# Attention scores and states' read by single heads in a fused attention and two-layer MoE kernel

## The chip, the cores and the metric

The kernel runs on one core of a Trainium2 chip. The metric is the device time of one execution in microseconds (us). The kernel before takes 1207.65 us, the median of 3 runs (1207.26 to 1207.77).

The engines are TensorE (PE, with its weight loads listed as PEld), VectorE (DVE), ScalarE (ACT), GpSimd (POOL) and SyncE (SP), which here only issues DMAs.

## The reference, cut to what matters

For each of 8 batches and 8 heads there are 512 tokens `x` and 32 states, each of 64 numbers. Tokens read the states, and the states read the tokens; both go on into two dense blocks.

```python
B, H, S, D = x.shape                      # 8, 8, 512, 64;  state: 8, 8, 32, 64
scores = scale * x @ state^T              # 512 x 32, softmax over the 32 states
xread  = softmax(scores) @ state
scores2 = scale * state @ x^T             # 32 x 512, softmax over the 512 tokens
sread  = softmax(scores2) @ x
h = concat([xread, sread], axis=2)        # 544 rows a head
# heads side by side: 4096 rows of tokens and 256 of states, 512 wide
y = ((h @ w1) * (h @ w2)) @ w3 @ w_out    # first block
g = y @ w_in;  out = (g * clip(g + 3, 0, 6) / 6) @ w_out2
```

`scores2` is the transpose of `scores`, so the kernel computes one product for both.

## The kernel before, in words

**The whole.** A first stage (0 to about 107 us) loads and unpacks weights and multiplies `w3` with `w_out` (line 463), while the attention of batches 0 and 1 is done in small pieces between the weights. Then a main loop runs over the batches b, and in each over 8 slots m of the first block's width. A slot has 12 matmuls for `ps_ab` (lines 88 to 90, `mm3`: three products of rounded halves instead of one in full precision), a product of the two halves on ACT and DVE (`asb`, `ab`, lines 571 and 573), its split into a high part `abh` (ACT) and a low part `abl` (DVE), and 12 matmuls into `x2` with it, one slot or two later. After batch 7 comes `s_block` for the states' 256 rows, then the second dense block (lines 996, 1158), which fills the rest of the span.

**The attention.** `attention(b)` is a generator. The main loop of batch b advances `attention(b + 1)` by one step at a time: after the `ps_ab` matmuls of a slot, and in the middle of a slot's `x2` matmuls. For batches 0 and 1 (`fine`) the steps are called from the first stage. Its parts, in order:

- `scores(g)` for a half g of the heads (four heads, two pairs): one matmul for each pair of heads. The stationary operand is a block diagonal `br[:, c, :]` of 128 rows (two heads' 64 numbers) and 64 columns (two heads' 32 states), the moving one `xr[:, c, :]` with 512 tokens. Two pairs make up one PSUM bank. For each half, `scores_out` takes the maximum on DVE, transposes 32x32 blocks on DVE for the tokens' own softmax (`sN`), and on ACT writes the exponentials `e2` and their sum `r2`.
- `max_n`, `exp_n`, `sum_n`, `div_n`: the tokens' softmax. `exp_n` also divides the states' exponentials: two ACT instructions of 128x512 (line 294) multiply `e2` with `1 / sum`.
- `e2_t`: eight TensorE transpositions of 128x128 turn `e2` into two banks `ps_e`, which ACT copies to `e2t` (tokens on partitions).
- `sread`: 32 matmuls into one bank `ps_r`. Stationary is `xn` (128 tokens x 64 numbers of one head), moving is `e2t` (128 tokens x 32 states). `sread_out` copies the bank to `xs` on ACT, and SP stores it; for batch 7 it goes to `xs_r`, which is split at once into `xs_hl`, the operand of `s_block`.

`p_mm(v)` multiplies a batch's states with `w1` and `w2`; its matmuls are 64 rows by 32 columns with 256 moving columns, eight of which stand beside each other in the array, and they use `br` too. Its results `ps_p` are split into `ph` (ACT) and `pl` (DVE).

**The order.** All engines run their instructions in the order in which the code writes them. PSUM has 8 banks: four for accumulation (`acc`: `ps_w`, `x2`), and a pool "b" of four, from which `ps_ab`, `ps_s`, `ps_e`, `ps_r`, `ps_p` and `ps_sb` take a bank as soon as an older tile's last reader is done. A step that holds a bank longer moves the tiles behind it to other banks.

A matmul in full 32-bit floats shows as two records in the trace; so `scores` of one batch are 8 records, `sread` 64, a `p_mm` 32. A transposition is one record.

Of the kernel before, what the change touches and what calls it, by code (L numbers as in the profile page):

```python
# [7 lines left out]
F32 = mybir.dt.float32  # L8
# [4 lines left out]
AF = mybir.ActivationFunctionType  # L13
# [3 lines left out]
DRAM = bass.MemoryType.DRAM  # L17


def attn_moe_kernel(tc, xt_d, xn_d, bd_d, wa, wb, wc, wi, wo, out):  # L20

# [15 lines left out]
    nc = tc.nc  # L39
    B, H, S, D, NS = 8, 8, 512, 64, 32  # L40
    DM, F1, F2 = 512, 1024, 2048
    T = S // 128
# [4 lines left out]
    scale = 1.0 / float(D) ** 0.5  # L47
# [5 lines left out]
    def open_pool(key, **kw):  # L53
        es[key] = ExitStack()
        return es[key].enter_context(tc.tile_pool(name=key, **kw))
# [10 lines left out]
    def bank(name):  # L66
        return psum.tile([128, 512], F32, tag="b", name=name, bufs=4)
# [32 lines left out]
    w12 = {}  # L100
# [7 lines left out]
    mid = open_pool("mid", bufs=1, side=left)  # L108
    ident = mid.tile([128, 128], F32, name="ident")
    att = open_pool("att", bufs=1, side=right)  # L110
# [99 lines left out]
    x_t, A_t, st_t = {}, {}, {}  # L210
    xs_r, xs_hl = None, []
    room = 0

    def load_x(b):
        xr = att.tile([128, 4, 512], F32, tag="xr", name=f"xr{b}")
        br = mid.tile([128, 4, 64], F32, tag="br", name=f"br{b}", bufs=2)
        nc.sync.dma_start(out=br, in_=bd_d[b])
        nc.sync.dma_start(out=xr, in_=xt_d[b])
        x_t[b] = (xr, br)

    def attention(b, fine=False):

        xr, br = x_t.pop(b)
        st_t[b] = br
        xn = att.tile([128, T, DM], F32, tag="xn", name="xn")
        nc.sync.dma_start(out=xn, in_=xn_d[b])
        sN = att.tile([128, 2, 512], F32, tag="sN", name="sN")
        e2 = att.tile([128, 2, 512], F32, tag="e2", name="e2")
        mr = att.tile([128, 32], F32, tag="mr", name="mr", bufs=2)
        m2, r2 = mr[:, :2], mr[:, 2:4]  # L230

        def scores(g):

            ps = bank("ps_s")
            for j in range(2):
                c = 2 * g + j
                nc.tensor.matmul(ps[64 * j:64 * j + 64], br[:, c, :], xr[:, c, :], start=True, stop=True)  # L237
            return ps

        def scores_out(g, ps):  # L240
            nc.vector.tensor_reduce(out=m2[:, g:g + 1], in_=ps, op=ALU.max, axis=AX.X)
            nc.vector.tensor_scalar(out=m2[:, g:g + 1], in0=m2[:, g:g + 1], scalar1=-scale, scalar2=None, op0=ALU.mult)
            nc.vector.transpose(out=sN[:, g, :], in_=ps)
            nc.scalar.activation(out=e2[:, g, :], in_=ps, func=AF.Exp, bias=m2[:, g:g + 1], scale=scale,
                                 accum_out=r2[:, g:g + 1])
# [12 lines left out]

        def sread():
            ps = bank("ps_r")  # L260
            for c in range(4):
                g, j = divmod(c, 2)
                for t in range(T):
                    for r in range(2):
                        h = 64 * r
                        o = 64 * j + NS * (r ^ g)
                        nc.tensor.matmul(ps[h:h + 64, c * NS:(c + 1) * NS], xn[:, t, c * 128 + h:c * 128 + h + 64],  # L267
                                         e2t[:, t, g, o:o + NS], start=(t == 0), stop=(t == T - 1))
            return ps

        def sread_out(ps):
            if b == B - 1:
                nc.scalar.copy(out=xs_r[:, :, b * NS:], in_=ps[:, :4 * NS].rearrange("p (c n) -> p c n", c=4))
                t = att.tile([128, T, DM], F32R, tag="xn", name="xs_hl").rearrange("p (i a) f -> p i (a f)", i=2)
                xs_hl.extend(t[:, i].rearrange("p (k f) -> p k f", k=KD) for i in range(2))
                rnd(xs_hl[0], xs_r, "A")
                rest(xs_hl[1], xs_r, xs_hl[0], "V")
                return
            xs = att.tile([128, 4, NS], F32, tag="xs", name="xs")
            nc.scalar.copy(out=xs.rearrange("p c n -> p (c n)"), in_=ps[:, :4 * NS])  # L280
            nc.sync.dma_start(out=xsd[:, :, b * NS:(b + 1) * NS], in_=xs)

        def max_n():
# [6 lines left out]

        def exp_n():
            nc.scalar.activation(out=sN, in_=sN, func=AF.Exp, scale=scale)
            for g in range(2):
                nc.scalar.activation(out=e2[:, g, :], in_=e2[:, g, :], func=AF.Copy, scale=r2[:, g:g + 1])

        def sum_n():
            nc.vector.tensor_reduce(out=sm[:, :, 0], in_=sv, op=ALU.add, axis=AX.X)
# [11 lines left out]
        sv = sN.rearrange("p g (k n) -> p (g k) n", n=NS)  # L309
        yield  # L310
        if fine:
            ps = scores(0)
            yield
            scores_out(0, ps)
            yield
            ps = scores(1)
            yield
            scores_out(1, ps)
        else:
            ps = [scores(g) for g in range(2)]  # L320
            for g in range(2):
                scores_out(g, ps[g])
            yield
# [7 lines left out]
        e2t = att.tile([128, T, 2, 128], F32, tag="xtl", name="e2t")  # L331
        sm = att.tile([128, 32, 1], F32, tag="sm", name="sm", bufs=2)
        if fine:
            ps = e2_t(0)
            yield
            e2_out(0, ps)
            sum_n()
            yield
            ps = e2_t(1)
            yield  # L340
            e2_out(1, ps)
            div_n()
            yield
            ps = sread()
            yield
            sread_out(ps)
            aT = att.tile([128, 2, 512], F32, tag="e2", name="aT")
            turn(aT)
        else:
            sum_n()  # L350
            yield
            div_n()
            yield
            yield
            ps = [e2_t(u) for u in range(2)]
            for u in range(2):
                e2_out(u, ps[u])
            yield
            aT = att.tile([128, 2, 512], F32, tag="e2", name="aT")
            turn(aT)  # L360
# [7 lines left out]
        rest(A_l, aT, A_h, "V")  # L368
        if not fine:
            yield  # L370
            sread_out(sread())

    live = []

# [11 lines left out]
    with tc.manual_schedule():  # L386
        make_identity(nc, ident)
        ps = bank("ps_i")
# [10 lines left out]
        def p_mm(v):  # L399
            b, mm = divmod(v, 4)  # L400
            ps = p_ps[v] = [bank("ps_p") for c in range(2)]

            for i in range(2):
                o = 512 * i + 256 * (mm % 2)
                for q in range(4):
                    for c in range(2):
                        j, k = divmod(q, 2)
                        r = slice(64 * (k ^ c), 64 * (k ^ c) + 64)
                        nc.tensor.matmul(ps[c][32 * q:32 * q + 32, 256 * i:256 * i + 256],  # L409
                                         st_t[b][r, 2 * c + j, 32 * k:32 * k + 32],  # L410
                                         w12[mm // 2, 2 * c + j][r, o:o + 256], start=True, stop=True)

        def p_split(v):
            ps = p_ps.pop(v)
# [384 lines left out]
        for b in range(B):  # L799
# [15 lines left out]
            for m in range(0 if b else 4, M1):  # L815
# [22 lines left out]
                if b == B - 2 and m >= 2:  # L838
                    if m == 2:
                        xs_r = wsq.tile([128, KD, SR], F32, name="xs_r")  # L840
                        n = (B - 1) * NS
# [124 lines left out]
        st = {}  # L966
# [306 lines left out]
def _layout(x, state, moe_w1, moe_w2, moe_w3, moe_w_out, moe2_w_in, moe2_w_out):  # L1273
    import numpy as np

    def words(a):
        return np.ascontiguousarray(a).view(np.uint64)

    B, H, S, D = x.shape
    NS = state.shape[2]  # L1280

    x6 = x.reshape(B, 4, 2, 4, 128, D)
    xt = x6.transpose(0, 2, 5, 1, 3, 4).reshape(B, 128, 4, 512)
    xn = x6.transpose(0, 4, 3, 1, 2, 5).reshape(B, 128, 4, 512)
    st = state.reshape(B, 4, 2, NS, D).transpose(0, 2, 4, 1, 3)
    bd = np.zeros((B, 2, D, 4, 2, NS), state.dtype)
    for c in range(4):
        for r in range(2):
            bd[:, r, :, c, r ^ c // 2, :] = st[:, r, :, c, :]
    wa = moe_w_out.reshape(4, 2, 128, 512).transpose(0, 2, 1, 3).reshape(4, 128, 1024)  # L1290
    w3t = moe_w3.T.reshape(8, 128, 2, 4, 128)
    wb = np.concatenate([w3t[:, :, 0].reshape(4, 2, 128, 512).transpose(0, 2, 1, 3).reshape(4, 128, 1024),
                         w3t[:, :, 1].transpose(2, 1, 0, 3).reshape(4, 128, 1024)])
    w12 = np.stack([moe_w1, moe_w2]).reshape(2, 4, 128, 2, 512)
    wc = w12.transpose(3, 1, 2, 0, 4).reshape(2, 4, 128, 1024)
    wi = moe2_w_in.reshape(2, 2, 128, 2, 8, 128).transpose(4, 2, 3, 0, 1, 5)
    wo = moe2_w_out.reshape(2, 8, 128, 4, 2, 2, 32).transpose(1, 2, 4, 0, 5, 3, 6).reshape(8, 128, 2, 2, 2, 128)
    wi, wo = (np.stack([w[:, :, 0, 1], w[:, :, 1, 1], w[:, :, 0, 0], w[:, :, 1, 0]], 2).reshape(8, 128, 1024)
              for w in (wi, wo))
    return {  # L1300
        "xt": np.ascontiguousarray(xt), "xn": np.ascontiguousarray(xn),
        "bd": bd.reshape(B, 128, 4, 64),
        "wa": words(wa), "wb": words(wb), "wc": words(wc), "wi": words(wi), "wo": words(wo),
    }

# [18 lines left out]
```

## Time and profile before

| What | Value |
|---|---|
| Median of 3 runs | 1207.65 us |
| The profiled execution | 1205.57 us |
| Its span, first to last instruction | 1203.8 us |
| PE busy | 1185.6 us, 98% of the span |
| DVE busy | 862.1 us, 72% |
| ACT busy | 553.5 us, 46% |
| Mean share of the 16 DMA engines, main loop from 220 us | 54% |
| Granted clock of TensorE | 0.996 |

Busy time of PE is made from ends that are modelled, so where instructions stand close the time of a group is read from its first start to the start of what follows. Time that an engine waits stands in brackets behind a row, with the engine and tile that ended the wait.

### The profile page before, as it was taken

How to read it: one execution, taken by the hardware profiler on the slowest of the kernel's cores; microseconds unless marked ns; L12 is line 12 of the kernel's file. 1: busy time of each engine (PE TensorE's matmuls, PEld its weight loads, DVE VectorE, ACT ScalarE, POOL GpSimd, SP SyncE). 2: the span in 40 equal slices, each digit the busy share in tenths (PEclk: the TensorE clock that was granted, in tenths of full speed). 3: DMA queues.
4: the chain of work that ended last, by engine and by line, in shares of the span. 5: the costliest groups of instructions: out<-in, count | busy, mean ns of one | idle time of the engine just before them, and what ended most of it. 6: DMA issues, size and time to landing. Idle time of an engine off the chain costs nothing.

```text
span 1203.8 us, 17243 instructions
## 1 busy us (share of the span) xinstructions
PE 1185.6 (98%) x6734; PEld 944.4 (78%) x6734; DVE 862.1 (72%) x1230; ACT 553.5 (46%) x811; POOL 44.6 (4%) x59
## 2 busy tenths in 40 slices
PE   7999999999999999999999999999999999999997
PEld 4356777777777789888888888888888888888887
DVE  7997888897898663455677866688567886558483
ACT  3544556455555553344445434454344543334341
POOL 0000000000000000000101001010010100001100
PEclk8999999999999999999999999999999999999999
DMA  8773558576674502036989769897698976536973
GB/s 328 270 252 109 182 169 283 184 267 212 206 269 167 180 1 70 19 105 222 314 240 303 232 215 298 249 293 248 219 284 258 277 251 205 176 123 178 246 224 71
DMA packets 118930, 252.67 MB, mean 210 GB/s; under 512 B 45248, under 2 KB 63168, under 8 KB 112448
## 3 DMA queue, kind: packets, MB, share of 16 engines
q1 hardware_dynamic: 109552, 222.46, 54.1%
q0 software_dynamic: 7632, 27.79, 11.4%
q10 hardware_dynamic: 1664, 1.31, 0.3%
q8 instruction: 53, 0.87, 0.3%
q14 instruction: 29, 0.24, 0.1%
HBM read 182.39 MB, written 47.64 MB: 191 GB/s over the span
## 4 chain that ended last, share of the span: by engine, by line
PE 91%; DVE 5%; DMA 2%; ACT 1%; issue 0%; SPq 0%; ACTq 0%
PE ps L996 25%; PE ps_d L1158 25%; PE x L88 5%; PE x L89 5%; PE x L90 5%; PE ps_ab L88 4%; PE ps_ab L89 4%; PE ps_ab L90 4%; PE ps_p L409 2%; PE ps_w L463 2%; PE ps_hs L996 2%; PE ps_so L1171 2%; DMA raw<-in_wb_dram 1%; PE ps_r L267 1%; PE ps_s L237 1%; DMA swih<-sh 1%
## 5 line engine op out<-in xcount | busy, mean ns | idle before, releaser
L996 PE MATMUL ps<-xc,wah 128*128 128x512 f32 x512 | 157.8, 389 | 0.0
L79 DVE TENSOR_TENSOR hlj<-g,hlj 128x1024 fp32r<-128x1024 f32 x84 | 102.4, 1219 | 36.7 <-ACT hlj L71 33.6
L926 ACT ACTIVATE rl<-c,half 128x512 f32<-128x512 f32 x96 | 69.5, 724 | 117.0 <-DVE c L896 68.1
L996 PE MATMUL ps<-xc,wbh 128*128 128x512 f32 x384 | 118.2, 389 | 0.0
L1158 PE MATMUL ps_d<-hlj,wah 128*128 128x512 f32 x384 | 118.2, 389 | 0.0
L88 PE MATMUL x<-abh,w3ph 128*128 128x512 f32 (+1 forms) x288 | 112.2, 390 | 1.5 <-ACT abh L71 1.5
L71 ACT ACTIVATE hlj<-g 128x1024 fp32r<-128x1024 f32 x84 | 88.5, 1058 | 52.1 <-PE ps_d L1158 46.6
L996 PEld LDWEIGHTS ps<-xc,wah 128*128 128x128 f32 x512 | 95.7, 188 | 19.5
L89 PE MATMUL x<-abl,w3ph 128*128 128x512 f32 (+1 forms) x288 | 109.0, 378 | 0.2 <-DVE abl L79 0.2
L90 PE MATMUL x<-abh,w3pl 128*128 128x512 f32 (+1 forms) x288 | 108.9, 378 | 0.0
L89 PE MATMUL ps_ab<-Al,ph 128*128 128x512 f32 x256 | 99.8, 390 | 0.6 <-DVE Al L79 0.6
L88 PE MATMUL ps_ab<-Ah,ph 128*128 128x512 f32 x256 | 100.3, 392 | 0.0
L90 PE MATMUL ps_ab<-Ah,pl 128*128 128x512 f32 x256 | 99.7, 389 | 0.0
L996 PE MATMUL ps<-xc,wal 128*128 128x512 f32 x256 | 99.6, 389 | 0.0
L1158 PE MATMUL ps_d<-hlj,wbh 128*128 128x512 f32 x288 | 88.7, 389 | 0.0
L71 ACT ACTIVATE abh<-ab 128x512 fp32r<-128x512 f32 (+1 forms) x72 | 43.7, 607 | 88.9 <-DVE ab L573 88.9
L1158 PEld LDWEIGHTS ps_d<-hlj,wah 128*128 128x128 f32 x384 | 72.1, 188 | 15.0
L996 PEld LDWEIGHTS ps<-xc,wbh 128*128 128x128 f32 x384 | 72.0, 188 | 14.9
L573 DVE TENSOR_TENSOR ab<-ps_ab,asb 128x512 f32<-128x512 f32 x64 | 44.1, 689 | 46.2 <-PE ps_ab L90 43.0
L964 POOL DMA_DIRECT2D g<-g x41 | 35.6, 869 | 1074.9 <-DVE c L896 566.8
L996 PE MATMUL ps<-xc,wbl 128*128 128x512 f32 x192 | 74.7, 389 | 0.0
L1158 PE MATMUL ps_d<-hlj,wal 128*128 128x512 f32 x192 | 74.7, 389 | 0.0
(170 smaller groups left out, 2357.6 us busy)
## 6 DMA issues: line engine op xcount, KB each, us to landing
g<-g POOLq DMA_DIRECT2D x41, 512.0 KB, 6.9
wah<-swih SPq DMA_DIRECT2D x32, 512.0 KB, 4.2
wal<-swil SPq DMA_DIRECT2D x32, 512.0 KB, 5.4
wah<-swoh SPq DMA_DIRECT2D x32, 512.0 KB, 4.4
wal<-swol SPq DMA_DIRECT2D x32, 512.0 KB, 5.3
wbh<-swih SPq DMA_DIRECT2D x32, 384.0 KB, 5.0
wbl<-swil SPq DMA_DIRECT2D x32, 384.0 KB, 5.3
wbh<-swoh SPq DMA_DIRECT2D x32, 384.0 KB, 5.7
```

What stands on the lines that cost most here:

```text
L71: nc.scalar.activation(out=out_, in_=in_, func=AF.Copy)
L79: e.tensor_tensor(out=out_, in0=in_, in1=hi.bitcast(F32), op=ALU.subtract)
L88: nc.tensor.matmul(ps, lh, rh, start=first, stop=False)
L89: nc.tensor.matmul(ps, lh, rl, start=False, stop=False)
L90: nc.tensor.matmul(ps, ll, rh, start=False, stop=last)
L409: nc.tensor.matmul(ps[c][32 * q:32 * q + 32, 256 * i:256 * i + 256], st_t[b][r, 2 * c + j, 32 * k:32 * k + 32], w12[mm // 2, 2 * c + j][r, ...
L463: nc.tensor.matmul(w3_ps[m], t[:, o:o + 128], wout[k], start=k == 0, stop=k == M1 - 1)
L573: nc.vector.tensor_tensor(out=ab[:, :n], in0=psb[:, :n], in1=a[:, :n], op=ALU.mult)
L926: nc.scalar.activation(out=rl, in_=c, func=AF.Relu, bias=half, scale=sign / 6.0)
L964: nc.gpsimd.dma_start(out=to, in_=of, accum_op=ALU.add)
L996: nc.tensor.matmul(ps, u[:, k, :], v[:, k, :], start=first and k == 0 and i == 0, stop=k == 1 and i == 2, skip_group_check=True)
L1158: nc.tensor.matmul(d[name][q][:, f], a, x[:, k, f], start=i < 3 and n == 0 and z == 0, stop=n == NG - 1 and z == 2, skip_group_check=True)
```

## The change

The first operand list loses the block diagonal: `br` holds only the states (128 partitions x 4 pairs x 32 columns), so its DMA brings 512 bytes instead of 1 KB to a partition. Scores are computed head by head with eight matmuls on 64x32 tiles: row half r of the array and column group c; row half r writes bank r. Both halves are computed together, for batches 0 and 1 too. A bank now holds the heads of equal r, four of them.

The states' read has stationary and moving operand exchanged: stationary is a head's `e2t` (128 tokens x 32 states), moving its `xn` (128 x 64), four heads beside each other in the four column groups. It uses undivided exponentials. The division is done when the result (128x128) is copied out of PSUM (`sread_div`, two ACT instructions of 128x64), and one step later a TensorE transposition puts it into the second quarter of the same bank, from where it goes on as before. The two ACT instructions on `e2` in `exp_n` go. `p_mm` keeps shape and number of its matmuls, with the new places of heads.

```diff
-        br = mid.tile([128, 4, 64], F32, tag="br", name=f"br{b}", bufs=2)
+        br = mid.tile([128, 4, NS], F32, tag="br", name=f"br{b}", bufs=2)
...
-        def scores(g):
-            ps = bank("ps_s")
-            for j in range(2):
-                c = 2 * g + j
-                nc.tensor.matmul(ps[64 * j:64 * j + 64], br[:, c, :], xr[:, c, :], start=True, stop=True)
+        def scores():
+            ps = [bank("ps_s") for r in range(2)]
+            for c in range(4):
+                for r in range(2):
+                    h = slice(64 * r, 64 * r + 64)
+                    nc.tensor.matmul(ps[r][NS * c:NS * c + NS], br[h, c, :], xr[h, c, :], start=True, stop=True)
...
         def sread():
             ps = bank("ps_r")
-            for c in range(4):
-                g, j = divmod(c, 2)
+            for g in range(2):
                 for t in range(T):
-                    for r in range(2):
-                        h = 64 * r
-                        o = 64 * j + NS * (r ^ g)
-                        nc.tensor.matmul(ps[h:h + 64, c * NS:(c + 1) * NS], xn[:, t, c * 128 + h:c * 128 + h + 64],
-                                         e2t[:, t, g, o:o + NS], start=(t == 0), stop=(t == T - 1))
+                    for c in range(4):
+                        nc.tensor.matmul(ps[NS * c:NS * c + NS, 64 * g:64 * g + 64], e2t[:, t, g, NS * c:NS * c + NS],
+                                         xn[:, t, 128 * c + 64 * g:128 * c + 64 * g + 64], start=(t == 0),
+                                         stop=(t == T - 1))
             return ps
 
-        def sread_out(ps):
+        def sread_div(ps):
+            sr = att.tile([128, 128], F32, tag="sr", name="sr")
+            for g in range(2):
+                nc.scalar.activation(out=sr[:, 64 * g:64 * g + 64], in_=ps[:, 64 * g:64 * g + 64], func=AF.Copy,
+                                     scale=r2[:, g:g + 1])
+            return sr
+
+        def sread_out(ps, sr):
+            ps = ps[:, 128:256]
+            nc.tensor.transpose(ps, sr, ident)
...
         def exp_n():
             nc.scalar.activation(out=sN, in_=sN, func=AF.Exp, scale=scale)
-            for g in range(2):
-                nc.scalar.activation(out=e2[:, g, :], in_=e2[:, g, :], func=AF.Copy, scale=r2[:, g:g + 1])
...
         if not fine:
             yield
-            sread_out(sread())
+            ps = sread()
+            sr = sread_div(ps)
+            yield
+        sread_out(ps, sr)
```

Three places show what this does to the order of the instructions. The first is PE in batch 4's main loop, where the scores of batch 5 follow a `p_mm`; before, these are its rows from the last `p_mm` matmul on:

```order
L409 MATMUL ps_p_2756<-big3_504,br4_2005 32x256
L237 MATMUL ps_s_2779<-xr5_2560,br5_2561 64x512 [waits DMAHW4_49,DMAHW3_49,Activation_49]
L237 MATMUL ps_s_2779<-xr5_2560,br5_2561 64x512
L237 MATMUL ps_s_2782<-xr5_2560,br5_2561 64x512 [waits DVE_49]
L237 MATMUL ps_s_2782<-xr5_2560,br5_2561 64x512
L88 MATMUL x2_2_2342<-abh_2593,w3ph6_494 128x512
```

The same place now:

```order
L416 MATMUL ps_p_2786<-big3_506,br4_2025 32x256
L238 MATMUL ps_s_2809<-xr5_2586,br5_2587 32x512 [waits DMAHW4_49,DMAHW3_49,Activation_49]
L238 MATMUL ps_s_2810<-xr5_2586,br5_2587 32x512 [waits DVE_49]
L238 MATMUL ps_s_2809<-xr5_2586,br5_2587 32x512
L238 MATMUL ps_s_2810<-xr5_2586,br5_2587 32x512
...
L88 MATMUL x2_2_2368<-abh_2619,w3ph6_496 128x512
```

Four matmuls of 64 columns became eight of 32, in the tile shape of the `p_mm` ahead of them, and the wait for DVE (its `ab` of the slot, which reads the bank that is taken) moved from the third matmul to the second.

The second place is PE at the states' read of batch 5, later in the same loop; before, from the read to the start of the next slot's `x2`:

```order
L267 MATMUL ps_r_3173<-e2t_2959,xn_2737 64x32 [waits DMAHW3_49,Activation_49]
L267 MATMUL ps_r_3173<-e2t_2959,xn_2737 64x32 x31
...
L88 MATMUL ps_ab0_3224<-Ah_2547,ph_3036 128x512 [waits DVE_49]
...
L88 MATMUL ps_ab1_3231<-Ah_2547,ph_3036 128x512 [waits Activation_49]
...
L88 MATMUL x2_0_2894<-abh_3096,w3ph5_432 128x512
```

The same place now:

```order
L265 MATMUL ps_r_3205<-xn_2767,e2t_2991 32x64 [waits DMAHW3_49,Activation_49]
L265 MATMUL ps_r_3205<-xn_2767,e2t_2991 32x64 x31
...
L88 MATMUL ps_ab0_3256<-Ah_2573,ph_3068 128x512 [waits DVE_49]
...
L88 MATMUL ps_ab1_3263<-Ah_2573,ph_3068 128x512 [waits DVE_49]
...
L279 MATMUL ps_r_3205<-ident_73,sr_3238 128x128 [waits Activation_49]
L88 MATMUL x2_0_2926<-abh_3128,w3ph5_434 128x512
```

The transposition stands behind six `x2` and twelve `ps_ab` matmuls, and `ps_r` keeps its bank until then; the second `ps_ab` therefore takes the bank of `ps_p` and waits for DVE (its first `pl`), where it waited for ACT's copy of `ps_r`.

The third place is ACT around the same read, before:

```order
L71 ACTIVATE ph_3167<-ps_p_3150 128x512 [waits PE_49]
L280 COPY xs_3206<-ps_r_3173 128x128 [waits PE_49]
L571 COPY asb_3238<-ps_ab0_3224 128x512 [waits PE_49,Activation_49]
L71 ACTIVATE sh_3245<-w_2981 128x768 [waits DMAHW0_49,DMAHW1_49,DVE_49,Activation_49]
```

And now:

```order
L71 ACTIVATE ph_3199<-ps_p_3182 128x512 [waits PE_49]
L273 ACTIVATE sr_3238<-ps_r_3205,mr_2771 128x64 [waits PE_49]
L273 ACTIVATE sr_3238<-ps_r_3205,mr_2771 128x64
L577 COPY asb_3270<-ps_ab0_3256 128x512 [waits PE_49,Activation_49]
L288 COPY xs_3275<-ps_r_3205 128x128 [waits PE_49]
L71 ACTIVATE sh_3281<-w_3013 128x768 [waits DMAHW0_49,DMAHW1_49,DVE_49,Activation_49]
```

The copy of the read result moved behind the slot's `asb` and waits for the transposition; `sh` (a part of a weight's split, which has nothing to do with attention) is queued behind it.

## Rows read from the trace of the kernel before

**Rows 1.** Windows of the span: length, busy us and count by engine, clock, DMA.

```profile
core 0: us, PE busy (x) PEld busy (x) DVE busy (x) ACT busy (x) POOL busy (x), PEclk, DMA share, GB/s
...
73.00:106.00 33.00, 31.72 (x204) 19.95 (x202) 29.97 (x44) 12.62 (x22) 0.00 (x0) 1.00 0.48 169
...
173.00:220.00 47.00, 45.74 (x368) 34.59 (x367) 41.32 (x67) 25.17 (x42) 0.00 (x0) 1.00 0.69 231
220.00:455.00 235.00, 235.00 (x1784) 181.57 (x1783) 188.03 (x292) 128.53 (x209) 0.00 (x0) 1.00 0.54 182
```

**Rows 2.** Waits of PE: line waited for, total us, times, longest.

```profile
PE ps_ab L89 <- DVE Al L79: 0.6, 1, 0.6
```

**Rows 3.** Timeline, first stage's end: start, us, engine, line, out<-in [idle <-releaser].

```profile
105.16 0.69 DVE L573 TENSOR_TENSOR ab<-ps_ab,asb 128x512 f32<-128x512 f32 x1
106.56 0.49 PE L88 MATMUL x<-abh,w3ph 128*128 128x512 f32 x1 [1.46 <-ACT abh L71]
```

**Rows 4.** Timeline of PE, scores of half a batch (batch 1).

```profile
87.90 1.08 PE L237 MATMUL ps_s<-xr,br 128*64 128x512 f32 x4 [0.39 <-PE ps_ab L90]
88.91 0.50 PE L88 MATMUL x<-abh,w3ph 128*128 128x512 f32 x1
```

**Rows 5.** Timeline of PE, p_mm and the scores of batch 2.

```profile
137.10 1.09 PE L409 MATMUL ps_p<-big,br 64*32 64x256 f32 x32
138.13 1.94 PE L237 MATMUL ps_s<-xr,br 128*64 128x512 f32 x8
140.00 0.50 PE L88 MATMUL x<-abh,w3ph 128*128 128x512 f32 x1
```

**Rows 6.** Timeline of 137.10 to 137.16 us alone: that p_mm's first starts.

```profile
137.10 0.45 PE L409 MATMUL ps_p<-big,br 64*32 64x256 f32 x8
```

**Rows 7.** Timeline of all engines at the states' read of batch 5.

```profile
338.62 2.06 PE L267 MATMUL ps_r<-e2t,xn 128*64 128x32 f32 x64
340.61 0.50 PE L88 MATMUL x<-abh,w3ph 128*128 128x512 f32 x1
340.76 1.28 DVE L79 TENSOR_TENSOR pl<-ps_p,ph 128x512 fp32r<-128x512 f32 x2
342.10 0.40 PE L88 MATMUL ps_ab<-Ah,ph 128*128 128x512 f32 x1
```

**Rows 8.** Timeline of PE, four transpositions among ps_ab matmuls (batch 1).

```profile
117.00 0.39 PE L90 MATMUL ps_ab<-Ah,pl 128*128 128x512 f32 x1
117.23 0.60 PE L252 MATMUL ps_e<-ident,e 128*128 128x128 f32 x4
117.58 0.47 PE L88 MATMUL ps_ab<-Ah,ph 128*128 128x512 f32 x1
117.90 0.39 PE L89 MATMUL ps_ab<-Al,ph 128*128 128x512 f32 x1
```

**Rows 9.** Timeline of DVE behind batch 1's states' read.

```profile
125.90 1.29 DVE L79 TENSOR_TENSOR pl<-ps_p,ph 128x512 fp32r<-128x512 f32 x2 [1.29 <-ACT ph L71]
```

**Rows 10.** Timeline of ACT, DVE and PE between 173 and 220 us.

```profile
187.57 0.85 ACT L71 ACTIVATE sh<-w 128x768 fp32r<-128x768 f32 x1 [2.50 <-DMA swih<-sh]
...
204.56 1.32 ACT L294 ACTIVATE e<-e,mr 128x512 f32<-128x512 f32 x2
...
208.11 0.69 DVE L79 TENSOR_TENSOR abl<-ab,abh 128x512 fp32r<-128x512 f32 x1 [1.76 <-ACT abh L71]
...
219.40 0.66 PE L252 MATMUL ps_e<-ident,e 128*128 128x128 f32 x4 [1.26 <-DVE ab L573]
```

**Rows 11.** Timeline of DVE and PE at batch 4's transpositions.

```profile
261.97 0.69 DVE L79 TENSOR_TENSOR abl<-ab,abh 128x512 fp32r<-128x512 f32 x1 [0.80 <-ACT abh L71]
...
271.44 0.68 DVE L573 TENSOR_TENSOR ab<-ps_ab,asb 128x512 f32<-128x512 f32 x1
...
272.42 1.09 PE L252 MATMUL ps_e<-ident,e 128*128 128x128 f32 x8
```

**Rows 12.** Timeline at the start of s_block.

```profile
447.49 1.06 ACT L71 ACTIVATE xs_hl<-xs_r 128x1024 fp32r<-128x1024 f32 x1
...
448.58 1.22 DVE L79 TENSOR_TENSOR xs_hl<-xs_r,xs_hl 128x1024 fp32r<-128x1024 f32 x1 [1.42 <-ACT xs_hl L71]
...
454.14 0.28 PE L89 MATMUL ps_sb<-xs_hl,wsh 128*128 128x256 f32 x1
```

More of the change, by code (lines that the diff above doesn't have):

```diff
@@ L17, with attn_moe_kernel @@
 DRAM = bass.MemoryType.DRAM
-def attn_moe_kernel(tc, xt_d, xn_d, bd_d, wa, wb, wc, wi, wo, out):
+def attn_moe_kernel(tc, xt_d, xn_d, st_d, wa, wb, wc, wi, wo, out):
     nc = tc.nc
@@ L215, in load_x @@
         xr = att.tile([128, 4, 512], F32, tag="xr", name=f"xr{b}")
-        br = mid.tile([128, 4, 64], F32, tag="br", name=f"br{b}", bufs=2)
-        nc.sync.dma_start(out=br, in_=bd_d[b])
+        br = mid.tile([128, 4, NS], F32, tag="br", name=f"br{b}", bufs=2)
+        nc.sync.dma_start(out=br, in_=st_d[b])
         nc.sync.dma_start(out=xr, in_=xt_d[b])
@@ L260, in sread @@
             ps = bank("ps_r")
-            for c in range(4):
-                g, j = divmod(c, 2)
+            for g in range(2):
                 for t in range(T):
-                    for r in range(2):
-                        h = 64 * r
-                        o = 64 * j + NS * (r ^ g)
-                        nc.tensor.matmul(ps[h:h + 64, c * NS:(c + 1) * NS], xn[:, t, c * 128 + h:c * 128 + h + 64],
-                                         e2t[:, t, g, o:o + NS], start=(t == 0), stop=(t == T - 1))
-            return ps
-        def sread_out(ps):
+                    for c in range(4):
+                        nc.tensor.matmul(ps[NS * c:NS * c + NS, 64 * g:64 * g + 64], e2t[:, t, g, NS * c:NS * c + NS],
+                                         xn[:, t, 128 * c + 64 * g:128 * c + 64 * g + 64], start=(t == 0),
+                                         stop=(t == T - 1))
+            return ps
+        def sread_div(ps):
[7 more added lines that the diff above has]
+            nc.tensor.transpose(ps, sr, ident)
             if b == B - 1:
-                nc.scalar.copy(out=xs_r[:, :, b * NS:], in_=ps[:, :4 * NS].rearrange("p (c n) -> p c n", c=4))
+                nc.scalar.copy(out=xs_r[:, :, b * NS:], in_=ps.rearrange("p (c n) -> p c n", c=4))
                 t = att.tile([128, T, DM], F32R, tag="xn", name="xs_hl").rearrange("p (i a) f -> p i (a f)", i=2)
@@ L279, in sread_out @@
             xs = att.tile([128, 4, NS], F32, tag="xs", name="xs")
-            nc.scalar.copy(out=xs.rearrange("p c n -> p (c n)"), in_=ps[:, :4 * NS])
+            nc.scalar.copy(out=xs.rearrange("p c n -> p (c n)"), in_=ps)
             nc.sync.dma_start(out=xsd[:, :, b * NS:(b + 1) * NS], in_=xs)
@@ L311, in attention @@
         if fine:
-            ps = scores(0)
+            ps = scores()
             yield
-            scores_out(0, ps)
+            scores_out(0, ps[0])
             yield
-            ps = scores(1)
             yield
-            scores_out(1, ps)
+            scores_out(1, ps[1])
         else:
-            ps = [scores(g) for g in range(2)]
+            ps = scores()
             for g in range(2):
@@ L345, in attention @@
             yield
-            sread_out(ps)
+            sr = sread_div(ps)
             aT = att.tile([128, 2, 512], F32, tag="e2", name="aT")
@@ L370, in attention @@
             yield
-            sread_out(sread())
+            ps = sread()
+            sr = sread_div(ps)
+            yield
+        sread_out(ps, sr)
     live = []
@@ L404, in p_mm @@
                 o = 512 * i + 256 * (mm % 2)
[L405 to L411, printed above, removed]
+                for c in range(4):
+                    for r in range(2):
+                        h = slice(64 * r, 64 * r + 64)
+                        nc.tensor.matmul(ps[r][NS * c:NS * c + NS, 256 * i:256 * i + 256], st_t[b][h, c, :],
+                                         w12[mm // 2, c][h, o:o + 256], start=True, stop=True)
         def p_split(v):
@@ L1284, in _layout @@
     xn = x6.transpose(0, 4, 3, 1, 2, 5).reshape(B, 128, 4, 512)
[L1285 to L1289, printed above, removed]
+    st = state.reshape(B, 4, 2, NS, D).transpose(0, 2, 4, 1, 3).reshape(B, 128, 4, NS)
     wa = moe_w_out.reshape(4, 2, 128, 512).transpose(0, 2, 1, 3).reshape(4, 128, 1024)
@@ L1301, in _layout @@
         "xt": np.ascontiguousarray(xt), "xn": np.ascontiguousarray(xn),
-        "bd": bd.reshape(B, 128, 4, 64),
+        "st": np.ascontiguousarray(st),
         "wa": words(wa), "wb": words(wb), "wc": words(wc), "wi": words(wi), "wo": words(wo),
```

## The prediction

> **What bounds the kernel now.** I read the table by windows first. From 220 to 455 us PE is busy in 235.00 of 235.00 us, beside DVE with 188.03 [rows 1]: what PE saves there shortens the run, as long as DVE follows. The window 73 to 106 reads otherwise: DVE 29.97 of 33.00, PE 31.72 [rows 1], where "busy" PE is mostly PE early; its end shows who decides, since DVE multiplies `ab` at 105.16 and PE then stands 1.46 us until 106.56 for the high part of it [rows 3]. The window 173 to 220 has PE at 45.74 of 47.00; the missing time is one wait, 1.26 us before transpositions at 219.40, ended by DVE's `ab` [rows 1, 10]. From the list of waits, one more counts: 0.6 us for `Al` at 133 us [rows 2]. So PE's savings count at full price from 106.6 us on, except between 173 and 219.4, where another chain decides.
>
> **Scores.** Eight records in tiles of two took 138.13 to 140.00 = 1.87 us, four rounds [rows 5]; four records, two rounds, took 87.90 to 88.91 = 1.01 [rows 4]. The difference gives 0.43 us for a round of 512 columns and 0.15 fixed. Now eight tiles of 64x32 are to stand in one round: two rounds (two records a matmul) instead of four, -0.86. That eight such tiles do run together is in the trace: `p_mm` has this tile shape, eight of its records start within 60 ns [rows 6], and all 32 of 256 columns take 137.10 to 138.13 = 1.03 us [rows 5], which is four rounds at half of 0.43 and about 0.17 fixed. The scores now follow a `p_mm` of their own shape, so up to 0.17 more may go where the shape no longer changes; I take half: **-0.95 a batch**, bounds 0.86 to 1.03.
>
> It counts for batch 2 (138 us) and batches 4 to 7. For batches 0 and 1 it falls into the stretch before 106 us that DVE sets, for batch 3 (191 us) into the other chain: 0. Five times 0.95 = **-4.75**. The second bank's wait for DVE `ab` stands in front now; at batch 3 it may bind, under cover of that chain, and elsewhere `ab` is out before the `p_mm` ahead is through.
>
> **States' read.** 64 records took 338.62 to 340.61 = 1.99 us [rows 7]: 32 rounds of two tiles, (1.99 - 0.15) / 32 = 57 ns a round, though only 32 columns stream in each. Now four column groups with 64 columns make 16 rounds. A round's floor by streaming is 0.43 x 64 / 512 = 54 ns; I take 57, the round that is there: 16 x 57 ns + 0.15 = 1.06, **-0.93 a batch**. Here the shape (128 rows, 32 columns) isn't in the trace. Its nearest rows are the present two tiles of 128 rows side by side, and the four column groups of `p_mm`. Bounds: no gain (31 ns a record as now) and -0.93.
>
> The Trainium skill's page "TensorE: Matmul & The Clock Gate", section "Wait — 56ns, not 53.3ns?", states that matmul starts never come closer than some 25 ns however few columns stream. By that, 64 records would take 1.6 us and the gain would be 0.24 instead of 0.93. The eight starts within 60 ns [rows 6] speak against this rule for records on different tiles, so I don't follow it.
>
> It counts for batch 1 (120.5 us) and batches 3 to 7, six times, **-5.58**. At batch 1 the time is kept, though PE waits for `Al` behind it: that chain begins with DVE standing 1.29 us for `ph`, made from the `p_mm` behind the read [rows 9], so it moves along. Batch 0 is under DVE, batch 2 (177 us) in the other chain.
>
> **The transposition.** One more full-array instruction a batch. Four of them, from 117.23, with the longer step behind them (117.58 to 117.90 instead of 0.23) cost 0.35 + 0.09 = 0.44, 0.11 each [rows 8]. A lone one pays more of what is fixed: 0.2, bounds 0.11 and 0.44. It counts for batches 3 to 7, **+1.00**; that of batch 1 falls into the 0.6 us of [rows 2], those of 0 and 2 are covered. Its input, ACT's two copies of 128x64, has the six `x2` and twelve `ps_ab` matmuls of some 4 us ahead of it.
>
> **The held bank.** `ps_r` stays a step longer, so the second `ps_ab` takes the bank of the first `ps_p` and waits for DVE's first `pl`. At batch 5 DVE did both from 340.76 in 1.28, so the first ended near 341.4. The first `ps_ab` began at 342.10 [rows 7] and the second six matmuls of 0.23 later, 343.5; 0.93 earlier it is 342.5. That leaves 1.1 us: 0.
>
> **ACT's division.** Two instructions, 1.32 us [rows 10], go from each `exp_n`; two small ones on the read result come, where ACT has idle time. In the main loop ACT is at 128.53 of 235 [rows 1], so mostly nothing. Between 173 and 219.4 it is on the path: ACT waits for a DMA until 187.57, the work behind goes through DVE to the tokens' exponentials on ACT, then the two divisions at 204.56, `sh`, `abh`, and DVE, idle 1.76 us, starts `abl` at 208.11; from there DVE works through to the `ab` that PE waits for at 219.40 [rows 10]. Taking out 1.32 brings `abl` forward by that (DVE has 1.76 to give), and the wait ends 1.3 earlier: **-1.30**. PE arrives 1.9 - 0.2 earlier there itself, so this chain still decides.
>
> **DVE after that.** At batch 4, `ab` ended at 272.12 and the second four transpositions began about half of 1.0 us behind 272.42: slack 0.8 [rows 11]. Between its scores and this point PE gains 0.95; DVE gains the 0.80 that it waited for ACT at 261.97 [rows 11], which was behind the divisions. 0.
>
> **s_block.** For batch 7 the result now comes a slot later: transposition, copy to `xs_r`, split on ACT 1.06, on DVE 1.22 [rows 12], needed by the matmul that was at 454.14. With the transposition near 451.4 in the old clock, this ends near 454.3: **+0.2**, bounds 0 and 0.5. The rest of the stores and the halved `br` DMA: not on PE's path, 0.
>
> **Sum.** -4.75 - 5.58 + 1.00 - 1.30 + 0.20 = -10.43. From the profiled execution's 1205.57 (span 1203.8 and 1.8 around it) that is 1195.1. The median of the runs is 2.1 above the profiled one, so I forecast 1207.65 - 10.43 = **1197.2**. With the bounds of scores and transposition its own range is 1195.5 to 1199.0.
>
> **Rivals.**
> A. *The read doesn't get shorter.* PE may be held by records, not by columns: 31 ns a record now, 32 ns on average in `p_mm` [rows 5, 7], nothing sustained denser. Then six gains of 0.93 go: 1207.65 - 4.85 = 1202.8. For it: no stretch in the trace refutes it over 64 records. Against: [rows 6], and weight loads of half as many columns. (By the page's 25 ns it would be six gains of 0.24: 1201.3.) 12%.
> B. *DVE and ACT keep the old pace.* The waiting copy on ACT pushes `sh` and `abh` back, so that the 1.3 at 204.56 isn't handed on and at the later batches PE gains only its slack of 0.8 against 0.95, four times 0.15: 1197.2 + 1.3 + 0.6 = 1199.1; if all four scores' gains (3.8) are lost to such waits, 1202.3. For it: the 1.26 us wait shows that DVE can hold PE. Against: ACT idles 2.5 us in that very place, waiting for a DMA [rows 10]. 13%.
> C. *Slower: 32-column tiles of 128 rows don't run beside each other.* Then the read is 64 passes of 57 ns one behind the other, 3.8 us instead of 1.99: six times +1.8 instead of -0.93, 16.4 in all, 1213.6. It decides from 41 ns a pass on: scores, ACT and s_block leave 4.85 us of gain behind the transpositions, 0.81 for each of six reads. Against: two tiles of 128 rows overlap now. 5%.
> D. *Nothing comes through*, since the same DVE chain sets all periods: within 0.2%, about what a measurement of this kernel can tell from no change (2.4 us). 3%.
>
> **How the numbers follow.** The forecast with its own range 61%, 6% below it (transpositions at 0.11, a gain from the chain at 173 us), A 12%, B 13%, D 3%, C 5%. Faster by over 0.2%: 61 + 6 + 12 + 13 = 92%; same 3%, slower 5%. The range takes in A and B: 1194.5 to 1203.0.
>
> **What would show it.** Right: scores in about 0.9 us between starts; the read's 64 records in 1.0 to 1.1; one `ident` record a batch costing PE about 0.2; the wait before the transpositions of batch 3 still there, ended near 218; PE full from there to 455 less about 7 us. Wrong: a read of 1.7 us or more, new waits of PE at `ps_s`, `ps_ab` or `ps_e` in batches 4 to 7, or at `ps_sb` over 0.5 us.

## The result and the profile after

The changed kernel takes 1196.69 us, the median of 5 runs (1195.37 to 1199.85), against 1207.52 of the kernel before (1206.78 to 1207.77): a ratio of 0.9914, 95% interval 0.9898 to 0.9930, 10.8 us less. The forecast was 1197.2. In a second set the two were at 1197.54 (6 runs) and 1208.17 (17 runs), 0.9918 (0.9901 to 0.9934).

The profiled execution has a span of 1194.9 us. Its windows, with the columns of [rows 1] (the main loop now ends some 9 us earlier, so the fourth is cut at 446):

```profile
73.00:106.00 33.00, 30.25 (x209) 19.45 (x207) 29.83 (x44) 12.88 (x24) 0.00 (x0) 1.00 0.46 162
106.00:138.00 32.00, 31.39 (x286) 23.33 (x286) 22.83 (x37) 16.85 (x28) 0.00 (x0) 0.95 0.31 96
...
173.00:220.00 47.00, 46.39 (x384) 34.88 (x384) 41.82 (x67) 25.73 (x45) 0.00 (x0) 1.00 0.70 231
220.00:446.00 226.00, 225.79 (x1818) 174.73 (x1817) 185.72 (x289) 123.72 (x207) 0.00 (x0) 1.00 0.56 188
```

PE still fills the main loop, but for 0.2 us, and DVE does nearly the same work in 9 us less. In 73 to 106 DVE is as busy as before and PE less: the savings there turned into standing. New is the clock of 0.95 in 106 to 138; before, this window read

```profile
106.00:138.00 32.00, 30.62 (x270) 22.98 (x270) 23.00 (x37) 18.54 (x29) 0.00 (x0) 1.00 0.30 95
```

PE's rows for the scores of batch 2, the read of batch 5 and its transposition answer to [rows 5, 7]:

```profile
136.63 1.09 PE L416 MATMUL ps_p<-big,br 64*32 64x256 f32 x32
137.52 1.06 PE L238 MATMUL ps_s<-xr,br 64*32 64x512 f32 x16
138.51 0.50 PE L88 MATMUL x<-abh,w3ph 128*128 128x512 f32 x1
...
331.96 1.10 PE L265 MATMUL ps_r<-xn,e2t 128*32 128x64 f32 x64
332.99 0.50 PE L88 MATMUL x<-abh,w3ph 128*128 128x512 f32 x1
...
337.21 0.28 PE L279 MATMUL ps_r<-ident,sr 128*128 128x128 f32 x1
337.24 0.48 PE L88 MATMUL x<-abh,w3ph 128*128 128x512 f32 x1
```

Scores take 0.99 us instead of 1.87, and the `p_mm` ahead hands over after 0.89 instead of 1.03; the read takes 1.03 instead of 1.99.

The list of PE's waits (columns as in [rows 2]):

```profile
PE ps_w L469 <- DVE t L168: 5.5, 2, 3.4
PE ps_w L469 <- DVE w3pl L79: 3.2, 1, 3.2
PE x L88 <- ACT abh L71: 2.1, 1, 2.1
PE ps L1002 <- DMA wal<-swil: 1.4, 1, 1.4
...
PE ps_e L253 <- DVE ab L579: 0.6, 1, 0.6
PE ps_ab L89 <- DVE Al L79: 0.5, 1, 0.5
...
PE x L88 <- ACT x2s L83: 0.2, 1, 0.2
```

The stand for `abh` at the end of the first stage grew from 1.46 [rows 3] to 2.08, and what follows it is new (PE's rows, columns as in [rows 5], and two windows as above):

```profile
105.44 0.49 PE L88 MATMUL x<-abh,w3ph 128*128 128x512 f32 x1 [2.08 <-ACT abh L71]
...
107.43 0.63 PE L88 MATMUL x<-abh,w3ph 128*128 128x512 f32 x1
...
111.06 0.40 PE L88 MATMUL ps_ab<-Ah,ph 128*128 128x512 f32 x1
```

```profile
108.00:110.00 2.00, 2.00 (x7) 1.52 (x6) 0.00 (x0) 0.00 (x0) 0.00 (x0) 0.50 0.00 0
110.00:112.00 2.00, 2.00 (x9) 1.61 (x8) 0.00 (x0) 0.00 (x0) 0.00 (x0) 0.80 0.00 0
```

For between 3 and 4 us TensorE was granted half of its speed, 1.2 instead of 2.4 GHz.

**From step to step.** One execution's span says little at this size: PE's start behind that stand lies between 105.4 and 110.6 us in the twelve executions profiled, of both kinds of attention, since the first stage differs from execution to execution: its clock, for one, falls near 20 and 48 us in some and not in others. So I compare distances between starts of PE's instructions behind it. x is PE's start after the stand, r, s and e are the first read, score and transposition of `e2` of a batch (the number), end is the end of the span:

```
              before  scores alone  changed  changed again  p_mm twice  scores twice
x  to r1       13.94      15.10      15.56       15.58         13.94        13.92
r1 to s2       17.62      17.53      16.53       16.53         16.51        16.52
s2 to e2       26.13      25.26      25.26       25.26         25.26        26.15
r2 to s3       14.13      14.00      13.16       13.16         13.91        13.16
s3 to e3       26.13      25.26      25.76       25.70         26.02        26.34
e3 to r3       14.67      15.12      14.03       14.05         14.02        13.39
r3 to s4       14.13      14.00      13.16       13.18         13.18        13.18
s4 to e4       26.13      25.26      25.26       25.26         25.37        26.15
s5 to e5       26.13      25.71      25.72       25.75         25.76        26.15
s6 to e6       26.13      25.26      25.49       25.42         26.59        26.15
e6 to r6       12.97      13.12      13.47       13.51         13.46        13.00
r7 to end     758.67     759.95     759.43      758.58        757.88       758.65
x  to end    1097.2     1095.2     1089.5      1088.6        1088.6       1090.3
```

### The profile page after: what moved, and what is told of

Its sections match the earlier page's. It is cut to its first block, busy times and chain, and to the rows that moved or that the text cites. A ratio compares the mean times of both kernels' runs of the same rounds, so it can differ in the third digit from the quotient of the medians.

```text
span 1194.9 us, 17377 instructions
## 1 busy us (share of the span) xinstructions
PE 1173.2 (98%) x6806; PEld 935.5 (78%) x6806; DVE 861.3 (72%) x1230; ACT 547.0 (46%) x811; POOL 44.6 (4%) x59
## 4 chain that ended last, share of the span: by engine, by line
PE 85%; DVE 9%; DMA 4%; ACT 1%; issue 1%; SPq 0%; ACTq 0%; DVEq 0%
PE ps_d L1164 25%; PE ps L1002 25%; PE x L88 5%; PE x L89 4%; PE x L90 4%; PE ps_ab L88 4%; PE ps_ab L89 4%; PE ps_ab L90 4%; PE ps_p L416 2%; PE ps_hs L1002 2%; PE ps_so L1177 2%; DMA raw<-in_wa_dram 1%; DMA wal<-swil 1%; DVE big L168 1%; DVE big L166 1%
```

## The experiments

From the fourth on each was executed once: there the evidence is the distances, not the time.

**1. The changed kernel again**, the same file.

> The changed kernel once more, unaltered, as the partner of the runs beside it. Theory (its own earlier trace): PE stands about 2.1 us before 105.4 us because the shorter scores let it arrive earlier at a point that VectorE sets, and right behind that TensorE's granted clock falls to 0.5 for about 4 us, which costs 1.6 us; this must come back in every run. Also the 1.8 us stand for a weight's DMA near 577 us. Rival: one or both are chance of that one execution; then the clock row of 106 to 112 us reads 1.00 here and the span is some 1.5 us shorter.

1197.54 us. The stand (2.46 us between starts) and the fall of the clock came back, x to r1 15.58. The wait for a weight's DMA near 577 us came back with 0.7 us instead of 1.4; it is in four of the twelve executions, and r7 to end varies by 2 us without any order. So the DMA wait belongs to the execution; the clock's fall came back at its place here, but needn't (experiment 9).

**2. p_mm twice.**

```diff
-            for i in range(2):
+            for i in (0, 1, 0, 1) if v == 2 else (0, 1):
```

> The changed kernel with the third p_mm (v = 2, near 102 us) computed twice over, same result: 1.03 us of TensorE work that falls into the stand before 105.4 us. Theory: the stand of 2.5 us between starts shrinks to about 1.4, the granted clock stays at 1.00 from 106 to 112 us, and all behind comes 1.6 us earlier: 1.6 us less than the changed kernel, some 1195. Rival (the clock's fall has nothing to do with this stand, or is chance): no change in the clock row and the time stays within 0.5 us of the changed kernel's, or is longer by the added work of 1.0.

1197.71 us (6 runs; ratio to before 0.9915, 0.9901 to 0.9930): no gain that shows beside 1197.54. At its place the theory held. PE's rows and the window behind the stand:

```profile
105.72 1.96 PE L416 MATMUL ps_p<-big,br 64*32 64x256 f32 x64
108.88 0.50 PE L88 MATMUL x<-abh,w3ph 128*128 128x512 f32 x1 [1.21 <-ACT abh L71]
```

```profile
110.00:112.00 2.00, 2.00 (x10) 1.64 (x9) 0.76 (x2) 0.75 (x1) 0.00 (x0) 1.00 0.00 0
```

The clock stayed at 1.00 and x to r1 is 13.94, 1.64 less. But x to end is 1088.6, as in the changed kernel's second execution. 0.75 went at r2 to s3 and 0.32 at s3 to e3, where ACT got its `sh` late from the DMA (9.30 us from the first of two DMAs' issue to ACT's start in this execution, 8.35 and 8.30 in the two of the changed kernel), and 1.17 at s6 to e6, behind a DVE that had stood 1.30 us for a DMA (`sl<-w,sh`, ended by `swol<-sl`). These losses follow DMA landings of that execution, so it doesn't show that saving the clock is worth nothing in general. The medians of six runs each don't show the 1.6 us either; whether the clock fell in the runs without a trace is not on record. The forecast of some 1195 was missed.

**3. Scores alone.** The read, its copy and the two divisions as before, in the new order of heads:

```diff
+                        nc.tensor.matmul(ps[h:h + 64, c * NS:(c + 1) * NS], xn[:, t, c * 128 + h:c * 128 + h + 64],
+                                         e2t[:, t, r, c * NS:(c + 1) * NS], start=(t == 0), stop=(t == T - 1))
...
+            for g in range(2):
+                nc.scalar.activation(out=e2[:, g, :], in_=e2[:, g, :], func=AF.Copy, scale=r2[:, g:g + 1])
```

> The changed kernel with the states' read undone: 32 matmuls of 64-column stationary xn and 32 moving columns, the two divisions of 128x512 back on ScalarE, no transposition, the result copied right away; the scores stay as eight 64x32 tiles. Theory: scores are worth 0.87 a batch in batches 2 and 4 to 7, 4.4 us, and lose the 1.6 us of the clock's fall: 1.5 to 4.5 us less than before, some 1203 to 1206; the changed kernel is 6 to 8 us shorter than this. Rival (the read brings nothing in time and scores carry the gain): this run is within 2 us of the changed kernel.

1204.24 us (12 runs; 0.9963, 0.9953 to 0.9974): 3.9 less than before, 6.7 more than the changed kernel beside it. The table separates the terms. Scores take 0.87 from s to e, and 0.13 more ahead of s, where `p_mm` of the same tile shape runs into them: 1.00 a batch. From r to s the changed kernel has 0.84 less than this one; the read itself is 0.96 shorter, so the transposition costs 0.12.

It also prices the division. From ACT's `sh` (188.32 here) to the second four transpositions:

```profile
188.32 0.85 ACT L71 ACTIVATE sh<-w 128x768 fp32r<-128x768 f32 x1 [1.88 <-DMA swih<-sh]
...
220.16 0.66 PE L253 MATMUL ps_e<-ident,e 128*128 128x128 f32 x4 [1.66 <-DVE ab L570]
```

that is 31.84 us, as before (187.57 to 219.40, 31.83 [rows 10]). In the changed kernel the two rows are

```profile
185.34 0.85 ACT L71 ACTIVATE sh<-w 128x768 fp32r<-128x768 f32 x1 [2.44 <-DMA swih<-sh]
...
215.95 0.66 PE L253 MATMUL ps_e<-ident,e 128*128 128x128 f32 x4 [0.61 <-DVE ab L579]
```

30.61: the divisions were worth 1.23 there. In all other executions in which PE waits for DVE at this place, the stretch is 31.80 to 31.86 with them (three more) and 30.59 to 30.66 without (four more).

**4. The read's columns split in two.**

```diff
-            for g in range(2):
+            for o in range(0, 128, 32):
+                g = o // 64
...
-                                         xn[:, t, 128 * c + 64 * g:128 * c + 64 * g + 64], start=(t == 0),
+                                         xn[:, t, 128 * c + o:128 * c + o + 32], start=(t == 0),
```

> The changed kernel with each read matmul cut into two of 32 moving columns (same stationary loaded twice): 128 records instead of 64 and 32 rounds of four tiles instead of 16, the columns streamed unchanged. Theory that a round lasts as long as its columns stream: a round of 32 columns takes some 27 to 31 ns, and the read stays near 1.0 to 1.1 us. Rival that weight loads of 32 columns or the issue of eight instructions a round bound it at about 55 ns: 32 x 55 ns + 0.15 = 1.9 us. Rival of a floor of 25 ns from start to start: 128 records take 3.2 us.

1208.69 us in its one execution. Two of the reads in PE's rows:

```profile
286.00 1.30 PE L266 MATMUL ps_r<-xn,e2t 128*32 128x32 f32 x128
287.22 0.50 PE L88 MATMUL x<-abh,w3ph 128*128 128x512 f32 x1
...
338.14 1.16 PE L266 MATMUL ps_r<-xn,e2t 128*32 128x32 f32 x112
342.50 0.44 PE L266 MATMUL ps_r<-xn,e2t 128*32 128x32 f32 x16 [3.19 <-issue]
```

128 records take 1.22 us: with 0.15 fixed that is 33 ns for a round of four tiles and 32 columns, against 55 ns for 64 columns ((1.03 - 0.15) / 16). So the columns set the round, near enough, and 9.5 ns a record is far below any floor of 25 ns. Both rivals fall. In two of the seven reads behind x (batches 2 and 5) PE stood for "issue" as well (1.8 and 3.4 us between starts), which no read of 64 records does; what kept the records away is not shown. Behind the stand of batch 5 the clock fell:

```profile
344.00:346.00 2.00, 2.00 (x6) 1.55 (x5) 0.00 (x0) 0.00 (x0) 0.00 (x0) 0.50 1.07 384
```

That stand and the slow matmuls behind it made r5 to s6 6.3 us longer, most of the 8.7 us by which x to end (1097.3) exceeds the 1088.6 of the changed kernel.

**5. The kernel before with a longer stand.**

```diff
-            ab = ab_mul(*e_ps.pop(m), 512)
+            ab = ab_mul(*e_ps.pop(m), 512, 2 if m == 3 else 1)
```

The third argument says how many times `ab_mul` makes VectorE's product.

> The kernel before, with one product of VectorE (the fourth early `ab`, near 105 us, 0.69 us) computed twice, same result: TensorE then stands about 2.5 us between starts there instead of 1.83, as in the changed kernel, with nothing of the changed attention in it. Theory (the length of the stand decides whether the clock falls): the granted clock drops to 0.5 right behind, and from the start after the stand to the states' read of batch 1 it takes about 15.5 us instead of 13.94. Rival (something else in the changed kernel lowers it): 13.9 us and the clock row at 1.00.

1211.38 us. A miss: the stand was 2.58 us between starts, and the clock held (x to r1 13.94). The length of the stand alone doesn't decide.

**6. The same with four products, and with two once more.**

> The kernel before with the same product of VectorE (near 105 us) computed four times, same result: TensorE stands about 4.0 us between starts instead of 1.83. So far the clock fell behind a stand of 2.5 us in five executions and held in two, and held behind 1.6 to 1.9 us in three. Theory (a longer stand makes a fall likelier, chance decides near 2.5 us): here it falls, and from the start after the stand to the states' read of batch 1 it takes 15 us or more instead of 13.94. Rival (the fall belongs to the changed kernel, whatever the stand): 13.9 us and the clock at 1.00.

> The kernel before with that product computed twice, once more (stand 2.5 us). Theory (chance decides): 13.9 or about 15.1 to 15.6 us from the start after the stand to the read of batch 1; a fall here shows that the kernel before has it too once it stands as long. Rival (never without the changed attention): 13.9.

1210.18 and 1208.10 us. With four products PE stood 4.05 us, and the clock fell in the kernel before too:

```profile
110.58 0.50 PE L88 MATMUL x<-abh,w3ph 128*128 128x512 f32 x1 [3.67 <-ACT abh L71]
```

```profile
112.00:114.00 2.00, 2.00 (x6) 1.54 (x5) 0.45 (x1) 1.66 (x3) 0.00 (x0) 0.50 0.00 0
```

x to r1 15.42. With two it held again (2.59 us, 13.98). So the fall is no property of the changed attention. Over all executions: held behind 1.6 to 1.9 us (3 of 3), fell behind 4.05 (1 of 1), and behind 2.46 to 2.59 it fell in five and held in three. All five were among the six with new scores at 2.46, both others with old ones held; what decides there stays open.

Other stands of the same executions speak against the scores as what decides. In the first stage PE waits twice for DVE in every execution, near 20 and 48 us. At the second of these waits the clock held behind 3.18 us idle in the changed kernel's first execution (first two rows), and fell behind 1.88 us in that of experiment 7, with the old scores (last two):

```profile
47.70 2.84 PE L469 MATMUL ps_w<-wo,t 128*128 128x512 f32 x6 [3.18 <-DVE w3pl L79]
48.00:50.00 2.00, 2.00 (x6) 0.81 (x5) 1.97 (x4) 0.84 (x2) 0.00 (x0) 1.00 0.00 0
...
47.85 2.50 PE L461 MATMUL ps_w<-wo,t 128*128 128x512 f32 x3 [1.88 <-DVE w3pl L79]
48.00:50.00 2.00, 2.00 (x3) 0.82 (x4) 1.97 (x4) 0.99 (x3) 0.00 (x0) 0.58 0.00 0
```

So in this range neither the length of the wait nor the kind of scores decides by itself.

**7. The kernel before without the divisions** (the two instructions of line 294 are left out, and with them the states' division in the result).

> The kernel before without the two ScalarE instructions of 128x512 that divide the states' exponentials (this leaves that division out of the result). Theory: only the stretch from ScalarE's `sh` at 187.57 to the transpositions of batch 3 gets shorter, 30.6 us instead of 31.8, and nothing else moves by more than 0.2: -1.2 us in all. Rival 1: VectorE sets that stretch by itself, and it stays at 31.8. Rival 2: the division holds other batches too (VectorE waits 0.5 to 0.8 us for ScalarE at batches 4 and 5), and it is over 2 us.

1205.09 us, x to end 1096.0, 1.2 less than before, all of it from e3 to r3 (14.67 to 13.39); no other distance moved by over 0.02. As expected, but not proof by itself: the DMAs ahead of `sh` landed 1.1 us earlier in this execution (7.97 us from the first issue to ACT, 9.10 before), which would have taken most of that by itself. The 1.23 of experiment 3 doesn't hang on that.

**8. The transposition five times.**

```diff
-            nc.tensor.transpose(ps, sr, ident)
+            for _ in range(5):
+                nc.tensor.transpose(ps, sr, ident)
```

> The changed kernel with the transposition of the read result made five times over, same result. Theory (0.14 us for one, from the step from read to scores with and without it): four more cost 0.11 to 0.14 each, so the step from the start of a read to the next batch's scores is 13.6 to 13.75 us instead of 13.17. Rival (a lone transposition is free beside the matmuls around it): below 13.3. Rival (0.2 each, as forecast): 13.97.

1199.10 us. The step from r to s is 13.62 at r4, r5 and r6 instead of 13.16: four cost 0.46, 0.115 each. A lone one costs what one of four does.

**9. Scores twice.**

```diff
-            for c in range(4):
+            for c in range(4) if fine else (0, 1, 2, 3, 0, 1, 2, 3):
```

> The changed kernel with the eight score matmuls of batches 2 to 7 made twice, same result: two more rounds of 0.43 us. Theory: +0.86 at batches 2 and 4 to 7, and nothing at batch 3, where the chain over a DMA, ScalarE and VectorE sets the transpositions; that makes the stretch behind the first stage 4.3 us longer than the changed kernel's, less what VectorE's waits at batches 5 and 6 (0.3 to 0.6 us each) give back. Rival: batch 3's scores count as well, 5.2 us, and its wait for VectorE `ab` shrinks by nothing.

1199.44 us. From s to e it adds 0.89 at batches 2, 4 and 7. At batch 3 it adds 0.6, and e3 to r3 gives 0.65 back: nothing, as expected. PE's row shows the eight transpositions there without a wait between them:

```profile
216.41 1.29 PE L253 MATMUL ps_e<-ident,e 128*128 128x128 f32 x8
```

At batch 5 it adds 0.4, and at 6 0.7 less the 0.5 that e6 to r6 gives back. This execution's clock held (x to r1 13.92, behind the same 2.46 us), so it stands 3.3 us above the changed kernel without its clock's fall (1088.6 - 1.64 = 1087.0 against 1090.3). That is the 4.3 expected less 1.0 that the waits at batches 5 and 6 gave back: there the scores were not all worth their price.

## Why the prediction was right, point by point

**Scores, -0.95 a batch.** Measured -1.00, in the bounds: 0.87 by rounds, 0.13 of the 0.17 of the changing shape. Batch 3's were rightly counted at nothing (experiment 9).

**Read, -0.93.** Measured -0.96, 0.03 outside its bound: the round is 55 ns, the estimate by streaming plus 1, not the 57 taken. Rival A needed a bound of 31 ns a record; it is 16 here and 9.5 in experiment 4. The Trainium skill ("TensorE: Matmul & The Clock Gate", section "Wait — 56ns, not 53.3ns?") says that starts never come closer than about 25 ns, by which the gain would have been 0.24. For records on different column tiles these traces disagree, as the eight starts of [rows 6] did. Rival C needed column groups of 128 rows to go one behind the other; they don't.

**Transposition, +0.20.** Measured 0.12; the lower bound, from four of them in a row, was the price. Five of them: +0.6 instead of +1.0.

**Held bank, 0.** Right: no wait at the second `ps_ab` behind a read, r to s is 13.2 us in every batch from 2 to 6 of the changed kernel.

**Division, -1.30 between 173 and 219.4.** Measured -1.23. The profile shows more there, the shift of PE against the kernel before grows by 1.97 from r2 to r3. The rest, 0.75, is the DMAs ahead of `sh`: 8.35 us from the first issue to `sh` instead of 9.10. That isn't the change's: over twelve executions it took 7.97 to 11.05 us with the old read and 8.06 to 10.02 with the new one.

**DVE after that, 0.** This step failed, in size. Batch 4 was right (slack 0.8), and it was taken for all. At batch 5 and 6 the changed kernel loses 0.5 (s5 to e5), 0.2 (s6 to e6) and 0.5 (e6 to r6) in the table, 1.2 together: `x` waits for ACT's `x2s` copies at 304 (and its weights' load at 356), and at batch 6 the second four transpositions wait for DVE's `ab` and at 373.3 the weights' load for DVE's `pl`:

```profile
304.25 0.50 PE L88 MATMUL x<-abh,w3ph 128*128 128x512 f32 x1 [0.17 <-ACT x2s L83]
```

```profile
373.30 0.19 PEld L88 LDWEIGHTS ps_ab<-Ah,ph 128*128 128x128 f32 x1 [0.37 <-DVE pl L79]
```

That is rival B in small: as PE's work gets shorter, DVE and ACT come to be waited for. Scores made twice take these waits away again (experiment 9: 26.15 at batches 5 and 6 as at the others, and e6 to r6 13.00). New waits at `ps_e` and `ps_ab` in batches 4 to 7 were among the prediction's own signs of being wrong; they came, but cost 1.2 us and not the 1.9 to 5.1 of rival B.

**s_block, +0.2.** Measured 0: the one new wait is 0.16 us of a weights' load for DVE's `xs_hl`, and the first `ps_sb` matmul starts 8.11 us behind r7 instead of 8.94, earlier by all that read and transposition of batch 7 give. The rest, from there to the end, is 749.2 to 751.3 us in the twelve executions, with either read.

**What no step had: the clock.** I counted scores under DVE's cover before 106 us at nothing, and that is what they saved; but the time came back as a longer stand, and behind it the clock fell in five of six executions with these scores and that stand, 1.2 to 1.6 us each (x to r1). A saving at nothing could cost something here. That the longer stand is the cause is likely, not shown: it held behind all three shorter ones at this place, but also behind two as long with the old scores.

**The sum.** Without the fall, x to end went from 1097.2 to 1087.0 (changed again), -10.2, beside -10.43 forecast. The terms as measured: scores -5.0, read -5.8, transposition +0.6, division -1.2, waits for DVE and ACT +1.2: -10.2. That these meet the measured -10.2 takes two things more that cancel: the DMAs ahead of `sh`, 0.8 earlier, and the way from the first `ps_sb` to the end, 0.7 longer; both vary by more than that over the twelve executions. With the fall it is -8.6 (and -7.7 in the first execution, where the DMA wait near 577 us cost 1.6). The timed medians say -10.8 and -10.6, each with some 2 us of interval; the one profiled execution of the kernel before, at 1205.57, lies below all 17 runs of the second set, which start at 1206.21, so the difference of two profiled spans understates the change. That the forecast met the median to 0.5 us is therefore partly luck: an unforeseen 1.6 and 1.2 stand against it, and a kernel before whose profiled execution is shorter than all its timed runs, for a reason that no trace here shows. The lower end of the forecast's own range, 1195.5, doesn't follow from the bounds of scores and transposition: these give 1196.4 to 1198.9, which holds both medians.

## What to carry to other kernels

Read for each stage which engine's wait ends last before giving a saving a price; with that, records counted in rounds of tiles gave every TensorE term to 0.1 us. A saving that falls under another engine's cover is not free of consequence: it lengthens a stand of TensorE, and behind a longer stand the clock can fall. When PE gets faster by 3% in a loop with DVE at 80%, check the slack at every period, not at one.

## What was not expected of the hardware

- Behind the stand at the end of the first stage TensorE's granted clock fell to 0.5 for between 3 and 4 us in five of eight executions with 2.46 to 2.59 us between starts, in the one with 4.05, and in none of three with 1.9 or less; it cost 1.2 to 1.6 us. Elsewhere it held behind 3.18 us idle and fell behind 1.88.
- Tiles of 128 rows and 32 columns with different moving data run four beside each other: 55 ns a round for 64 columns, 33 ns for 32; two tiles of 64 columns took 57 ns for 32. With the same 32 columns streamed, the round with half the stationary columns (and four tiles instead of two) is the shorter one, so the old read was not bound by its streamed columns; that its weight loads bound it is likely, not shown.
- In two of seven reads of 128 records PE stood for "issue", 1.8 and 3.4 us between starts; in no read of 64.
